# RWKV attention with an expert layer on one core: other fillers on TensorE at the start, and the loads from item 3 on in half rows

## The chip, the cores and the metric

The program runs on one core of a Trainium2 chip. Its time is device microseconds of one execution, as the median over several runs. Engine names are those of the profile: PE is TensorE's products, PEld its loads of weights, DVE is VectorE, ACT ScalarE, POOL GpSimd, and SP the engine that here issues most transfers. A q behind a name means the engine's queue of issues.

## What is computed

An RWKV-5 attention is followed by a mixture of eight experts, all in float32.

```python
# attention: batch 4, 8 heads, 768 tokens, 48 values per head
for t in range(S):
    cur = np.einsum('bhd,bhe->bhde', u[None] * kt, vt)
    y[:, :, t] = np.einsum('bhd,bhde->bhe', rt, state + cur)
    state = w[None, :, :, None] * state + np.einsum('bhd,bhe->bhde', kt, vt)
# experts: x is y as (batch, token, 384); one expert e per token
    e = argmax(logits) if (s == 0 or local_gate < 0.5) else previous e
    h = np.maximum(x[b, s] @ w1[e], 0.0)          # 384 -> 1024
    out[b, s] = p[e] * (h @ w2[e])                # 1024 -> 384
```

## The kernel before, in words

Attention is cut into 16 **items**: one batch and one pair of heads each, four pairs for each of four batches. An item's 768 tokens are six chunks of 128. Within a chunk the recurrence is a matrix of scores; between chunks a state of 48 x 48 per head is carried. The work of an item, with the names that the profile shows:

- `load(n)` issues on SP the transfers of r and k by columns of heads (`rk`, 128 x 1536 values, 768 KB), of keys and values by tokens (`kv`, 128 x 1168, 584 KB) and of the values turned (`vT`, 128 x 768, 384 KB). There are four buffers for `rk` and `vT` and five for `kv`. Items 0 to 2 are loaded ahead of everything; item n + 3 is issued at the head of step n.
- `scale(n)` is POOL's share: `pd` = r times k (L219), `ke` = keys times powers of w to the end of the chunk (L215), and `rw` = r times powers of w (L236). For the items 0 to 2 DVE makes `rw`. Each of the three is two instructions. From item 3 on the order is rw, ke, pd, with item 4 as ke, rw, pd.
- `keys(n)` makes `kw` = k over powers of w on DVE (L246), and on POOL for the last two items.
- On PE: `scores` multiplies rw and kw into a pair of banks (L297), which DVE masks into `am` (L299); `own` is the token's own term, from pd and u (L276), and DVE multiplies it by vT (L282); `added` makes what each chunk adds to the state, from ke and v (L258), which DVE's scan `S` (L264) carries on; `inside` (L306) and `before` (L319) are the two products that make y; ACT copies y out (L327), and `turn` (L338) transposes it.

The powers of w stand in `tab` (and `end`, `endT`), made at the start from `w_t`, which holds w and u for the four pairs of heads. For pair 0 DVE makes them by a scan and for the three others POOL by doubling (L134). `ends` and `turn_ends` make the powers counted from the chunk's end: copies on ACT, two transposes on PE for each pair of heads (L175), and a copy of the result on ACT (L176).

Ahead of item 0's scores PE does **fillers** that nothing reads: `align(26)` is 26 products of 32 x 32, `warm(8)`, `warm(5)` and, ahead of `added(0)`, `warm(3)` are transposes of the unit matrix. A product in float32 is two loads of weights and two products in the profile's counts, a transpose one of each. `banks` hands out two pairs of PSUM banks by turns, to fillers too, so that a tenant waits until the one before the last has been read.

The order of the work is the order in which it is written, for each engine by itself; waits are set by what an instruction reads and overwrites. Besides, every transfer of SP and ACT takes one of eight semaphores by turns, and its issue waits until the transfer that had the semaphore before has landed.

The experts follow. Their tokens are collected by indirect transfers (`xg`) in POOL's queue, the weights `w1t` and `w2t` come by SP and ACT, and the products are L1159, L1209, L1246, L1278 and others.

Of the kernel before, what the change touches and what calls it, by code (L numbers as in the profile page):

```python
# [20 lines left out]
P = 128  # L21
B, H, S, DH = 4, 8, 768, 48
HP = H // 2
DP = 64
# [28 lines left out]
VB = NCH * 2 * DH  # L53
# [3 lines left out]
def spread(ap, axis, n):  # L57

    a = ap.unsqueeze(axis)
    return a.to_broadcast([n if i == axis else s for i, s in enumerate(a.shape)])  # L60


class Attention:
# [13 lines left out]
    def __init__(self, tc, st, rk_d, kv_d, vT_d, x_d, w_t, wp_d, kept, ident, lt, mp):  # L77
        self.tc, self.nc = tc, tc.nc
        nc = tc.nc
        self.rk_d, self.kv_d, self.vT_d, self.x_d = rk_d, kv_d, vT_d, x_d  # L80
        self.w_t, self.kept, self.ident, self.lt = w_t, kept, ident, lt

        self.late = st.enter_context(tc.tile_pool(name="late", bufs=1))
        self.wp = self.late.tile([P, H, 32], F32, name="wp")
        self.inner = ExitStack()

        def pool(name, bufs, **kw):
            return self.inner.enter_context(tc.tile_pool(name=name, bufs=bufs, **kw))

        once = pool("once", 1)  # L90
        self.two = pool("two", 2)
        self.four = pool("four", 4)
        self.py = pool("py", 1, space=PSUM)
        ps = pool("ps", 1, space=PSUM)

        self.pairs = [ps.tile([P, 2, 512], F32, name=f"pair{i}") for i in range(2)]

        self.T = mp[:, 2 * P + 2:2 * P + 2 + (NCH - 1) * DH].rearrange("p (e c) -> p e c", c=NCH - 1)

        self.inv = pool("pinv", 1, space=PSUM).tile([P, HP, P], F32, name="inv")  # L100


        n = B * HP - 1
        self.rks, self.vTs = [None] * AHEAD, [None] * AHEAD
        for i in range(1, AHEAD + 1):
            self.rks[(n + i) % AHEAD] = once.tile([P, 2, NCH, P], F32, name=f"rk{i}")
        for i in range(1, AHEAD + 1):
            self.vTs[(n + i) % AHEAD] = once.tile([P, 2, C2, P], F32, name=f"vT{i}")
        self.kvs = [once.tile([P, 2 * VB + DP - DH], F32, name=f"kv{i}") for i in range(AHEAD + 1)]
        self.items = [dict() for _ in range(B * HP)]  # L110
        self.xTs, self.xs, self.lTs = {}, {}, {}
        for i in range(AHEAD - 1):
            self.load(i)
        nc.sync.dma_start(out=self.wp, in_=wp_d)


        self.step = once.tile([P, HP, DH, NCH - 1], F32, name="step")
        nc.vector.memset(self.step, 0.0)


        self.tab = tab = once.tile([P, HP, 2, P + 1], F32, name="tab")
        nc.vector.memset(tab[:, 0, :, 0:1], 1.0)
        nc.gpsimd.memset(tab[:, 1:, :, 0:1], 1.0)
        w = once.tile([P, HP, 2], F32, name="w")
        nc.vector.tensor_scalar(w[:, :, 0], w_t[:, :, 0], W_LO, W_HI, Alu.max, Alu.min)
        nc.vector.reciprocal(w[:, :, 1], w[:, :, 0])
        none = self.step[:, 0, 0, 0:1].to_broadcast([P, P])
        for o in range(2):
            nc.vector.tensor_tensor_scan(tab[:, 0, o, 1:], w[:, 0, o:o + 1].to_broadcast([P, P]), none, 1.0, Alu.mult, Alu.add)
        nc.gpsimd.tensor_copy(tab[:, 1:, :, 1], w[:, 1:])  # L130
        n, t = 2, tab[:, 1:]
        while n <= P:
            m = min(n - 1, P + 1 - n)
            nc.gpsimd.tensor_mul(t[..., n:n + m], t[..., 1:1 + m], t[..., n - 1:n].to_broadcast([P, HP - 1, 2, m]))  # L134
            n += m

        self.first, self.newton = mp[:, :P + 1], mp[:, P + 1:2 * P + 1]
        nc.scalar.copy(self.first, tab[:, 0, 0])
        self.reciprocals(0)

        self.end = once.tile([P, HP, P + DP], F32, name="end")
        self.endT = once.tile([P, 2, HP, 2 * DH], F32, name="endT")
        self.align(26)
        self.warm(8)
        self.ends(slice(0, 1))
        self.turn_ends(slice(0, 1))
        self.warm(5)

    def align(self, n):

        t = self.banks("warm")
        for i in range(n):
            self.nc.tensor.matmul(t[:32, i % 2, :32], lhsT=self.ident[:, :32], rhs=self.ident[:, :32], start=True, stop=True)

    def reciprocals(self, i):

        nc, inv = self.nc, self.tab[:, i, 1, 1:]
        nc.vector.scalar_tensor_tensor(self.newton, self.first[:, 1:], -1.0, inv, Alu.mult, Alu.mult)
        nc.vector.scalar_tensor_tensor(self.inv[:, i], self.newton, 2.0, inv, Alu.add, Alu.mult)

    def warm(self, n):

        t = self.banks("warm")
        for i in range(n):
            self.nc.tensor.transpose(t[:, i % 2, :P], self.ident, self.ident)

    def ends(self, z):
        self.nc.scalar.copy(self.end[:, z, :P], self.tab[:, z, 0, P - 1::-1])
# [22 lines left out]
    def load(self, n):  # L191
        nc = self.nc
        b, hp = divmod(n, HP)
        rk, vT, kv = self.rks[n % AHEAD], self.vTs[n % AHEAD], self.kvs[n % (AHEAD + 1)]
        if n:
            nc.sync.dma_start(out=rk.rearrange("p a c t -> p (a c t)"), in_=self.rk_d[b, hp])
        else:
            for z in (slice(0, C2), slice(C2, NCH)):
                nc.sync.dma_start(out=rk[:, :, z], in_=self.rk_d[b, hp].rearrange("p (a c t) -> p a c t", a=2, c=NCH)[:, :, z])
        nc.sync.dma_start(out=kv, in_=self.kv_d[b, hp])  # L200
        nc.sync.dma_start(out=vT.rearrange("p a c t -> p (a c t)"), in_=self.vT_d[b, hp])
        self.items[n].update(b=b, hp=hp, rT=rk[:, 0], kT=rk[:, 1], vT=vT,
                             k=kv[:, :VB].rearrange("p (c x) -> p c x", c=NCH), v=kv[:, VB:])
# [158 lines left out]
    def run(self, router, fetch, heads):  # L362
# [11 lines left out]
        for n in range(M + 1):  # L374
            if n + AHEAD - 1 < M:
                self.load(n + AHEAD - 1)
            if n == 0:
                self.scale(0)
                self.keys(0)
                self.tables()  # L380
                self.scores(0, 0)()
                self.scores(0, 1)()
                self.nc.scalar.copy(self.first, self.tab[:, 1, 0])
                self.reciprocals(1)
                self.own(0)
                self.turn_ends(slice(1, HP))
                self.warm(3)
                self.added(0)
                self.states(0)
                self.scale(1)  # L390
                continue
# [133 lines left out]
def general_attention(tc, rk_d, kv_d, wu, wg_d, x_d, ident, lt):  # L525

    nc = tc.nc
    with tc.tile_pool(name="g1", bufs=1) as g1, tc.tile_pool(name="g2", bufs=2) as g2, \
# [8 lines left out]
        nc.vector.tensor_copy(turned[:, DP:], ident[:, :DP])  # L537
        with tc.For_i(0, HP, 1) as hp:
            wu_t = g1.tile([P, 2], F32, name="g_wu")
            nc.sync.dma_start(out=wu_t, in_=wu[bass.ds(hp, 1)].rearrange("o p x -> (o p) x"))  # L540
            with tc.For_i(0, B, 1) as b:
                def of(ap):
                    return ap[bass.ds(b, 1), bass.ds(hp, 1)].rearrange("o q p x -> (o q p) x")
# [7 lines left out]
                                  in_=of(kv_d)[:, 2 * NCH * DH:4 * NCH * DH])  # L551
                yp = gy.tile([P, 2, 512], F32, name="g_y")
                for e in range(DH):
                    vp = gps.tile([P, 2, 512], F32, name="g_vp")
                    for c in range(NCH):
                        for i in range(2):
                            nc.tensor.matmul(
                                vp[i * DP:(i + 1) * DP, c // 3, (c % 3) * P:(c % 3 + 1) * P],
                                lhsT=v_t[:, c, i, e:e + 1].to_broadcast([P, DP]),
                                rhs=turned if c % 2 else ident,  # L560
                                start=True, stop=True)
                    kv = g2.tile([P, S], F32, name="g_kv")
# [6 lines left out]
                    z = g2.tile([P, S], F32, name="g_z")  # L569
                    nc.vector.scalar_tensor_tensor(z, kv, wu_t[:, 1:2], sv[:, :S], Alu.mult, Alu.add)  # L570
                    nc.vector.tensor_mul(z, z, r_t)
                    for c in range(NCH):
                        o = (c % 3) * 2 * DH + 2 * e
                        nc.tensor.matmul(yp[:, c // 3, o:o + 2], lhsT=z[:, c * P:(c + 1) * P], rhs=ones,
                                         start=True, stop=True)
                y = g1.tile([P, 2, 3, 2, DH], F32, name="g_ys")
                for g in range(2):
# [5 lines left out]
                    out=x_d.rearrange("(b c p) (h j) -> b h p c j", b=B, p=P, h=HP)  # L583
                    [bass.ds(b, 1), bass.ds(hp, 1)].rearrange("o q p c j -> (o q p) c j"),
                    in_=y.rearrange("p g c i e -> p (g c) (i e)"))
    with tc.tile_pool(name="g3", bufs=2) as g3, tc.tile_pool(name="gl", bufs=3, space=PSUM) as gl:
        wg = g3.tile([P, DK, E + 1], F32, name="g_wg", bufs=1)
        nc.sync.dma_start(out=wg, in_=wg_d)
        for c in range(NC):
            x = g3.tile([P, D], F32, name="g_x")  # L590
# [7 lines left out]
            for kk in range(DK):  # L598
                nc.tensor.matmul(lp[:, :E + 1], lhsT=xT[:, kk * P:(kk + 1) * P], rhs=wg[:, kk, :],
                                 start=(kk == 0), stop=(kk == DK - 1))  # L600
# [362 lines left out]
def route(tc, once, ps, lt, ident, gates):  # L963
# [57 lines left out]
    nc.vector.tensor_copy(ccol, cp[:NC, :1])  # L1021
    run = tl("run", [NC, P])
    nc.vector.tensor_tensor_scan(run, rows, rows, ccol, Alu.max, Alu.max)
    rp = bank("rp")
    nc.tensor.transpose(rp[:, :NC], run, ident[:NC, :NC])
    ei = tl("ei", [P, NC], I32)
    nc.vector.tensor_copy(ei, rp[:, :NC])
# [635 lines left out]
def kernel(  # L1663
# [12 lines left out]
    nc = tc.nc  # L1676
# [2 lines left out]
    x_d = dram.tile([N, D], F32, name="x_d")  # L1679

    w_t = keep.tile([P, HP, 2], F32, name="w_t")
    nc.scalar.dma_start(out=w_t, in_=wu.rearrange("h p x -> p h x"))
    ident = keep.tile([P, P], F32, name="ident")
    make_identity(nc, ident)
    mask = keep.tile([P, P], F32, name="mask")
# [120 lines left out]
```

## Time and profile before

| | us |
|---|---|
| median of 3 runs | 377.63 |
| lowest and highest | 376.92 and 379.44 |
| the profiled execution, its own time | 378.4 |
| its span, first to last instruction | 376.7 |
| mean granted clock of TensorE | 0.996 |

The profiled execution is a run of its own, 0.8 us above the median; 1.7 us of it lie outside the span. The profile's rows name a line of the kernel, an engine, an operation, what is written and read (buffer numbers left out) and how many instructions were merged into the row (x). In a timeline the first two numbers are the start from the span's beginning and the duration, in us, and the bracket at the end is idle time of that engine just ahead, with what ended it; "issue" stands for a wait for nothing that the profile shows. In a row of the windows an engine has its busy time and, in brackets, its number of instructions; behind the engines come the granted clock, the share of time that the 16 DMA engines were busy, and what they moved.

### The profile page before, as it was taken

The page shows a single profiled execution, that of the slowest core. Times are in us where ns is not written, and L with a number is a line of the kernel's source. Part 1 is how long each engine was busy: PE and PEld are TensorE (multiplying, and loading weights), DVE is VectorE, ACT ScalarE, POOL GpSimd, SP SyncE. Part 2 cuts the span into 40 slices and gives each one's busy share as a digit, 9 for nine tenths or more (in the row PEclk, how much of TensorE's full clock was granted, in tenths as well). Part 3 has the DMA queues.
Part 4 walks back from the last instruction along what each step waited for, and adds up shares of the span by engine and source line. Part 5 has one row for each costly group of instructions (what it writes and reads, how often), then busy time and mean ns, then how long its engine had stood idle before and what let it go on. Part 6 is the DMA issues. An engine that isn't in the chain of part 4 may idle for free. (4 is left out here: it accounts for less than half of the span.)

```text
span 376.7 us, 9667 instructions
## 1 busy us (share of the span) xinstructions
PE 361.5 (96%) x3844; PEld 318.7 (85%) x3844; DVE 244.8 (65%) x711; ACT 110.5 (29%) x304; POOL 152.3 (40%) x212
## 2 busy tenths in 40 slices
PE   7998899999999999999999999999999999999992
PEld 6766777777769998989899999999999998989971
DVE  6887778788834835886557666857767767555300
ACT  4222232223523212322332233333243233331210
POOL 8789999789512055212333113313233023021012
PEclk9999999999999999999999999999999999999998
DMA  7999998992568748713352452264165065072011
GB/s 256 411 407 408 404 409 314 338 357 106 196 194 298 269 169 336 260 35 127 121 198 62 155 216 78 56 218 186 36 209 220 14 220 202 19 259 114 2 41 37
DMA packets 17764, 74.93 MB, mean 199 GB/s; under 512 B 2778, under 2 KB 6624, under 8 KB 15408
## 3 DMA queue, kind: packets, MB, share of 16 engines
q1 hardware_dynamic: 10336, 56.89, 40.7%
q0 software_dynamic: 3424, 9.48, 7.3%
q10 hardware_dynamic: 3952, 7.87, 5.6%
q8 instruction: 32, 0.52, 0.6%
q14 instruction: 20, 0.16, 0.1%
HBM read 64.79 MB, written 9.47 MB: 197 GB/s over the span
## 5 line engine op out<-in xcount | busy, mean ns | idle before, releaser
L1358 POOL DMA_INDIRECT out_dram<-yo,sid x27 | 26.6, 985 | 115.8 <-ACT yo L1353 92.3
L1209 PE MATMUL h<-exT,w1t 128*128 128x168 f32 (+4 forms) x240 | 54.9, 327 | 0.0
L1213 DVE TENSOR_TENSOR hT<-h,hs 128x168 f32<-128x168 f32 (+3 forms) x60 | 21.1, 351 | 46.2 <-PE h L1209 29.6
L1132 POOL DMA_INDIRECT xg<-x_d,gid x29 | 31.2, 1076 | 30.3 <-DVE gid L899 19.2
L1209 PEld LDWEIGHTS h<-exT,w1t 128*128 128x128 f32 x240 | 41.6, 190 | 0.3 <-issue 0.3
L1159 PE MATMUL h<-exT,w1t 128*128 128x168 f32 (+2 forms) x192 | 37.3, 332 | 0.0
L299 DVE TENSOR_TENSOR am<-pair,kept 128x768 f32<-128x768 f32 x32 | 30.1, 953 | 11.0 <-PE pair L297 10.8
L1278 PE MATMUL y<-factors,sums 128*128 128x192 f32 x168 | 36.8, 326 | 0.0
L219 POOL TENSOR_TENSOR pd<-rk 128x384 f32<-128x384 f32 x32 | 31.8, 1014 | 8.9 <-PE y L276 6.3
L1209 PE MATMUL h<-xs,ws 128*128 128x168 f32 (+4 forms) x144 | 35.3, 327 | 0.0
L1159 PEld LDWEIGHTS h<-exT,w1t 128*128 128x128 f32 x192 | 30.9, 190 | 2.0 <-issue 0.2
L1278 PEld LDWEIGHTS y<-factors,sums 128*128 128x128 f32 x168 | 29.0, 190 | 0.2
L1209 PEld LDWEIGHTS h<-xs,ws 128*128 128x128 f32 x144 | 25.5, 190 | 4.3 <-ACT hs L1216 1.2
L297 PE MATMUL pair<-rw,kw 48*64 48x128 f32 (+1 forms) x768 | 23.4, 249 | 1.9 <-issue 1.7
L236 POOL TENSOR_TENSOR rw<-rk,tab 128x384 f32<-128x384 f32 x26 | 23.6, 930 | 0.4 <-DMA rk<-in_rk_dram 0.4
L306 PE MATMUL y<-am,kv 128*64 128x128 f32 x360 | 22.9, 276 | 0.3
L1278 PE MATMUL y<-w2t,hT 128*128 128x192 f32 x96 | 23.0, 328 | 0.0
L297 PEld LDWEIGHTS pair<-rw,kw 48*64 48x64 f32 x768 | 19.9, 133 | 3.4 <-issue 2.4
L1146 DVE COPY exT<-tp 128x384 f32<-128x384 f32 (+5 forms) x29 | 13.8, 485 | 13.2 <-PE tp L1145 13.1
L215 POOL TENSOR_TENSOR ke<-kv,endT 128x288 f32<-128x288 f32 (+1 forms) x32 | 21.8, 704 | 0.9 <-DMA kv<-in_kv_dram 0.9
L306 PEld LDWEIGHTS y<-am,kv 128*64 128x64 f32 x360 | 19.4, 137 | 2.2 <-issue 1.1
L327 ACT COPY xT<-y 128x768 f32<-128x768 f32 x15 | 12.0, 801 | 29.0 <-PE y L319 29.0
(304 smaller groups left out, 735.4 us busy)
## 6 DMA issues: line engine op xcount, KB each, us to landing
w1t<-in_w_dram SPq DMA_DIRECT2D x8, 1536.0 KB, 6.9
w2t<-in_w_dram SPq DMA_DIRECT2D x8, 1536.0 KB, 7.4
rk<-in_rk_dram SPq DMA_DIRECT2D x15, 768.0 KB, 10.3
kv<-in_kv_dram SPq DMA_DIRECT2D x16, 584.0 KB, 8.5
vT<-in_vT_dram SPq DMA_DIRECT2D x16, 384.0 KB, 6.3
x_d<-x ACTq DMA_DIRECT2D x4, 1152.0 KB
w1t<-in_w_dram SPq DMA_DIRECT2D x2, 768.0 KB
w2t<-in_w_dram SPq DMA_DIRECT2D x2, 768.0 KB, 5.2
```

The lines of the kernel that those rows point to most:

```text
L215: nc.gpsimd.tensor_mul(t["ke"][:, z], t["k"][:, z], spread(self.endT[:, p, hp], 1, len(range(NCH)[z])))
L219: nc.gpsimd.tensor_mul(t["pd"][:, z], t["rT"][:, z], t["kT"][:, z])
L236: engine.tensor_mul(t["rw"][:, z], t["rT"][:, z], spread(pw, 1, z.stop - z.start))
L297: nc.tensor.matmul(sc[f * DP:(f + 1) * DP, h, i, x:], lhsT=t["kw"][q, c, o * DP:(o + 1) * DP], rhs=t["rw"][q, c, x:], start=True, stop=True)
L299: return lambda: nc.vector.tensor_mul(t["am"][:, g], sc, spread(self.kept[:, g:g + 3], 1, 2))
L306: nc.tensor.matmul(t["y"][h][p * DP:(p + 1) * DP, c2 * P:(c2 + 1) * P], lhsT=t["v"][:, (2 * c + h) * DH:(2 * c + h) * DH + DP], rhs=t["am" ...
L1132: self.nc.gpsimd.indirect_dma_start(out=xg[:n], out_offset=None, in_=self.x_d[:rows], in_offset=bass.IndirectOffsetOnAxis(ap=u["gid"][:n, ...
L1159: nc.tensor.matmul(h[:, :n], lhsT=u["w1"][:, m, kk, :], rhs=u["xT"][:, kk, :], start=(kk == 0), stop=(kk == DK - 1))
L1209: nc.tensor.matmul(out, lhsT=a, rhs=b, start=start and k == 0, stop=stop and k == len(terms) - 1, skip_group_check=True)
L1213: nc.vector.tensor_tensor(out, a, b, op=Alu.add)
L1278: return lambda: nc.tensor.matmul(bank[:, x * half:(x + 1) * half], lhsT=a, rhs=b, start=(j == 0 and x == 0), stop=(j == FK // 2 - 1), ski ...
L1358: self.nc.gpsimd.indirect_dma_start(out=out.rearrange("n (h d) -> (n h) d", h=2) if half else out, out_offset=bass.IndirectOffsetOnAxis(ap ...
```

## The change

Three things change.

The fillers are now products of the unit matrix with three copies of itself, 384 columns wide: three ahead of the two transposes for pair 0 and one behind. The three transposes ahead of `added(0)` go, and the six transposes of the other pairs move ahead of `own(0)`.

From item 3 on `rk` comes as two transfers, r and then k, and `kv` as two, keys and then values. The rows are then 3,072 bytes for r and k, 2,304 for keys and 2,368 for values, where they were 6,144 and 4,672. `vT` stays whole.

The array of w and u is laid out by partition on the host, so that each partition reads 32 bytes in one piece; before it read four pieces of 8 bytes.

```diff
-        self.align(26)
-        self.warm(8)
+        self.fill(3)
         self.ends(slice(0, 1))
         self.turn_ends(slice(0, 1))
-        self.warm(5)
+        self.fill(1)
...
+    def fill(self, n):
         t = self.banks("warm")
         for i in range(n):
-            self.nc.tensor.matmul(t[:32, i % 2, :32], lhsT=self.ident[:, :32], rhs=self.ident[:, :32], start=True, stop=True)
+            self.nc.tensor.matmul(t[:, i % 2, :3 * P].rearrange("p (c t) -> p c t", c=3), lhsT=self.ident,
+                                  rhs=spread(self.ident, 1, 3), start=True, stop=True)
...
-        if n:
+        if n > 2:
+            for a in range(2):
+                nc.sync.dma_start(out=rk[:, a].rearrange("p c t -> p (c t)"), in_=self.rk_d[b, hp][:, a * S:(a + 1) * S])
+            for a in range(2):
+                z = slice(a * VB, VB if a == 0 else 2 * VB + DP - DH)
+                nc.sync.dma_start(out=kv[:, z], in_=self.kv_d[b, hp][:, z])
+        elif n:
             nc.sync.dma_start(out=rk.rearrange("p a c t -> p (a c t)"), in_=self.rk_d[b, hp])
...
-        nc.sync.dma_start(out=kv, in_=self.kv_d[b, hp])
+        if n <= 2:
+            nc.sync.dma_start(out=kv, in_=self.kv_d[b, hp])
...
                 self.reciprocals(1)
+                self.turn_ends(slice(1, HP))
                 self.own(0)
-                self.turn_ends(slice(1, HP))
-                self.warm(3)
                 self.added(0)
...
-    nc.scalar.dma_start(out=w_t, in_=wu.rearrange("h p x -> p h x"))
+    nc.scalar.dma_start(out=w_t, in_=wu)
...
-        "wu": _np.stack([w, u.reshape(HP, P)], 2),
+        "wu": _np.stack([w, u.reshape(HP, P)], 2).transpose(1, 0, 2),
```

PE's first rows before the change. `pair` is one of the two pairs of banks, with its number; x26 counts the products as the kernel writes them:

```order
1 L153 MATMUL pair_149<-ident 32x32 x26
2 L165 MATMUL pair_148<-ident 128x128 x8
3 L175 MATMUL pair_149<-ident,end 128x128 x2
4 L165 MATMUL pair_148<-ident 128x128 x5
5 L297 MATMUL pair_149<-rw,kw 64x128 x12
6 L297 MATMUL pair_148<-rw,kw 64x128 x12
7 L276 MATMUL y<-pd,w_t 64x384 x4
8 L175 MATMUL pair_149<-ident,end 128x128 x6
9 L165 MATMUL pair_148<-ident 128x128 x3
10 L258 MATMUL mp<-kv_162,ke 64x48 x10
```

And the same place of PE's program after it (the lines of the source have moved):

```order
1 L152 MATMUL pair_149<-ident 128x384 x3
2 L169 MATMUL pair_148<-ident,end 128x128 x2
3 L152 MATMUL pair_149<-ident 128x384
4 L298 MATMUL pair_148<-rw,kw 64x128 x12
5 L298 MATMUL pair_149<-rw,kw 64x128 x12
6 L169 MATMUL pair_148<-ident,end 128x128 x6
7 L277 MATMUL y<-pd,w_t 64x384 x4
8 L259 MATMUL mp<-kv_162,ke 64x48 x10
```

The first scores still take the banks that the two transposes used, and `own(0)` now stands behind the other six transposes.

SP's loads of the items 3 and 4 before the change, with what each issue waits for; DMAHW0 to 7 are the eight semaphores of the transfers:

```order
11 L196 DMA rk_157<-in_rk_dram 128x1536 [waits DMAHW4_49]
12 L200 DMA kv_165<-in_kv_dram 128x1168 [waits DMAHW5_49]
13 L201 DMA vT_161<-in_vT_dram 128x768 [waits DMAHW6_49]
14 L196 DMA rk_154<-in_rk_dram 128x1536 [waits DMAHW7_49,DVE_49,Pool_49]
15 L200 DMA kv_166<-in_kv_dram 128x1168 [waits DMAHW0_49]
16 L201 DMA vT_158<-in_vT_dram 128x768 [waits DMAHW1_49,DVE_49]
```

And after it:

```order
11 L191 DMA rk_157<-in_rk_dram 128x768 [waits DMAHW4_49]
12 L191 DMA rk_157<-in_rk_dram 128x768 [waits DMAHW5_49]
13 L194 DMA kv_165<-in_kv_dram 128x576 [waits DMAHW6_49]
14 L194 DMA kv_165<-in_kv_dram 128x592 [waits DMAHW7_49]
15 L202 DMA vT_161<-in_vT_dram 128x768 [waits DMAHW0_49]
16 L191 DMA rk_154<-in_rk_dram 128x768 [waits DMAHW1_49,DVE_49,Pool_49]
17 L191 DMA rk_154<-in_rk_dram 128x768 [waits DMAHW2_49]
18 L194 DMA kv_166<-in_kv_dram 128x576 [waits DMAHW3_49]
19 L194 DMA kv_166<-in_kv_dram 128x592 [waits DMAHW4_49]
20 L202 DMA vT_158<-in_vT_dram 128x768 [waits DMAHW5_49,DVE_49]
```

An item is five transfers where it was three, and each still waits for the eighth before it.

More of the change, by code (lines that the diff above doesn't have):

```diff
@@ L142, in __init__ @@
         self.endT = once.tile([P, 2, HP, 2 * DH], F32, name="endT")
-        self.align(26)
-        self.warm(8)
+        self.fill(3)
         self.ends(slice(0, 1))
         self.turn_ends(slice(0, 1))
-        self.warm(5)
-    def align(self, n):
+        self.fill(1)
+    def fill(self, n):
         t = self.banks("warm")
         for i in range(n):
-            self.nc.tensor.matmul(t[:32, i % 2, :32], lhsT=self.ident[:, :32], rhs=self.ident[:, :32], start=True, stop=True)
+            self.nc.tensor.matmul(t[:, i % 2, :3 * P].rearrange("p (c t) -> p c t", c=3), lhsT=self.ident,
+                                  rhs=spread(self.ident, 1, 3), start=True, stop=True)
     def reciprocals(self, i):
@@ L159, in reciprocals @@
         nc.vector.scalar_tensor_tensor(self.inv[:, i], self.newton, 2.0, inv, Alu.add, Alu.mult)
[L161 to L165, printed above, removed]
     def ends(self, z):
@@ L539, in general_attention @@
             wu_t = g1.tile([P, 2], F32, name="g_wu")
-            nc.sync.dma_start(out=wu_t, in_=wu[bass.ds(hp, 1)].rearrange("o p x -> (o p) x"))
+            nc.sync.dma_start(out=wu_t, in_=wu[:, bass.ds(hp, 1)].rearrange("p o x -> p (o x)"))
             with tc.For_i(0, B, 1) as b:
```

## The prediction

> **What bounds the kernel now.** I read the windows first, since the program has two stages with different limits.
>
> ```profile
> core 0: us, PE busy (x) PEld busy (x) DVE busy (x) ACT busy (x) POOL busy (x), PEclk, DMA share, GB/s
> 3.00:4.00 1.00, 1.00 (x23) 1.00 (x22) 0.95 (x4) 0.26 (x2) 0.51 (x3) 1.00 1.00 307
> 10.00:15.00 5.00, 5.00 (x125) 4.49 (x126) 3.95 (x7) 1.61 (x3) 3.62 (x5) 1.00 1.02 415
> ...
> 200.00:300.00 100.00, 100.00 (x630) 95.23 (x629) 69.14 (x229) 32.24 (x91) 24.67 (x31) 1.00 0.38 134
> ```
>
> From 200 to 300 us PE is busy all the time, with DMA at 0.38: the experts are bound by products. Nothing in the change touches them, so what it is worth is how much earlier or later attention hands over to them. Up to 57 us the picture is another: the 16 DMA engines have no free time (share 1.02). An item is 768 + 584 + 384 KB, 1.78 MB, so 4.4 us at 408 GB/s. The timeline of POOL shows who waits for these loads, that of PE who does not:
>
> ```profile
> 8.79 1.55 POOL L215 TENSOR_TENSOR ke<-kv,endT 128x288 f32<-128x288 f32 x2
> 11.34 1.96 POOL L219 TENSOR_TENSOR pd<-rk 128x384 f32<-128x384 f32 x2 [1.01 <-DMA rk<-in_rk_dram]
> 16.02 1.97 POOL L219 TENSOR_TENSOR pd<-rk 128x384 f32<-128x384 f32 x2 [1.39 <-DMA rk<-in_rk_dram]
> 20.63 1.69 POOL L236 TENSOR_TENSOR rw<-rk,tab 128x384 f32<-128x384 f32 x2 [0.42 <-DMA rk<-in_rk_dram]
> 23.59 1.97 POOL L219 TENSOR_TENSOR pd<-rk 128x384 f32<-128x384 f32 x2
> 26.49 1.35 POOL L215 TENSOR_TENSOR ke<-kv,endT 128x288 f32<-128x288 f32 x2 [0.94 <-DMA kv<-in_kv_dram]
> 45.49 1.97 POOL L219 TENSOR_TENSOR pd<-rk 128x384 f32<-128x384 f32 x2 [0.81 <-PE y L276]
> ```
>
> POOL waits for loads of items 1 to 4 only. From 26.49 it needs 1.69 + 1.35 + 1.97 = 5.0 us an item, more than the 4.4 us of a load, so the loads run ahead; at 45.49 its first later wait is for PE. And PE, in the timeline of its weight loads, stands still in the middle of groups with no releaser:
>
> ```profile
> 26.77 0.54 PEld L297 LDWEIGHTS pair<-rw,kw 48*64 48x64 f32 x23 [0.44 <-issue]
> 33.43 0.54 PEld L297 LDWEIGHTS pair<-rw,kw 48*64 48x64 f32 x22 [1.09 <-issue]
> 39.77 0.30 PEld L258 LDWEIGHTS mp<-kv,ke 128*48 128x48 f32 x9 [1.47 <-issue]
> 51.93 0.48 PEld L258 LDWEIGHTS mp<-kv,ke 128*48 128x48 f32 x17 [0.52 <-issue]
> 57.53 0.44 PEld L258 LDWEIGHTS mp<-kv,ke 128*48 128x48 f32 x16 [0.24 <-issue]
> ```
>
> The windows cut at these halts (and at 46.0, where no halt is seen) count what PE did between them:
>
> ```profile
> 26.76:33.42 6.66, 5.64 (x126) 4.47 (x127) 5.82 (x7) 1.50 (x3) 6.66 (x9) 1.00 1.02 408
> 33.42:39.76 6.34, 4.99 (x126) 3.11 (x125) 4.61 (x6) 0.48 (x1) 6.34 (x8) 1.00 1.03 412
> 39.76:46.00 6.24, 6.23 (x126) 4.97 (x126) 3.60 (x23) 1.50 (x3) 5.42 (x8) 1.00 1.01 399
> 45.99:51.92 5.93, 5.54 (x130) 4.37 (x129) 4.86 (x7) 2.94 (x12) 5.86 (x8) 1.00 1.04 410
> 51.92:57.52 5.60, 5.48 (x126) 4.32 (x127) 3.93 (x6) 1.22 (x3) 4.64 (x6) 1.00 1.03 409
> 57.52:62.60 5.08, 5.07 (x125) 3.81 (x128) 4.17 (x7) 1.21 (x3) 4.72 (x7) 1.00 0.93 344
> ...
> PE 361.5 (96%) x3844; PEld 318.7 (85%) x3844; DVE 244.8 (65%) x711; ACT 110.5 (29%) x304; POOL 152.3 (40%) x212
> ...
> q1 hardware_dynamic: 10336, 56.89, 40.7%
> q10 hardware_dynamic: 3952, 7.87, 5.6%
> q8 instruction: 32, 0.52, 0.6%
> ```
>
> Products and weight loads add up to 251 to 259 each time, and the DMA queue called instruction moved 32 pieces, 0.52 MB / 32 = 16 KB each. PE ran 3,844 + 3,844 instructions, 240 for each of 32 pieces. I infer that PE's program comes in pieces of about 256 instructions through the same busy DMA engines, and that while these are full a piece takes 5.6 to 6.7 us to come. So **from 20 to 57 us PE is paced by its own program**; the halts add up to 0.44 + 1.09 + 1.47 + 0.52 + 0.24 = 3.8 us. At DMA share 0.93 the piece takes 5.08 us and nothing halts.
>
> **The change, part by part.** *The front on PE.* The rows of the start:
>
> ```profile
> 1.55 2.98 PE L153 MATMUL pair<-ident 128*32 128x32 f32 x52 [1.55 <-POOL ident masks.py:199]
> 3.01 0.17 DVE L125 TENSOR_SCALAR w<-w_t 128x4 f32<-128x4 f32 x1 [1.05 <-DMA w_t<-in_wu_dram]
> 4.46 1.17 PE L165 MATMUL pair<-ident 128*128 128x128 f32 x8
> 5.69 0.71 PE L165 MATMUL pair<-ident 128*128 128x128 f32 x5
> 6.31 0.55 DVE L236 TENSOR_TENSOR rw<-rk,mp 128x384 f32<-128x384 f32 x1
> 6.33 1.54 PE L297 MATMUL pair<-rw,kw 48*64 48x128 f32 x48
> 10.39 0.49 PE L165 MATMUL pair<-ident 128*128 128x128 f32 x3
> 10.81 0.79 PE L258 MATMUL mp<-kv,ke 128*64 128x48 f32 x20
> ...
> 252.25 0.81 PE L1285 MATMUL tp<-w2t,hT 128*120 128x384 f32 x2
> 252.90 0.32 PE L1209 MATMUL h<-xs,ws 128*128 128x188 f32 x1
> ```
>
> A product of 384 columns in f32 is two instructions; the pair at 252.25 held PE for 0.65 us. Three fillers end at 1.55 + 1.95 = 3.5 us, against 5.4 for the old ones, which held back the two transposes behind them. Their copy frees the bank for the first scores, which can then start when the first half of rw is there (5.9) instead of 6.33. That does not carry far: the second half of rw ends at 6.86 as before. Then the three transposes at 10.39 go, and own(0) changes places with the six transposes of the other pairs of heads. What is late next for the added states (10.81) is ke(0), which POOL ends at 10.34: they start at 10.4, a gain of **0.4 us** for PE and for DVE's scan behind them. own(0) still waits for pd(0), and DVE's product behind it isn't moved.
>
> *w and u by whole rows of a partition.* 512 pieces of 8 bytes become 128 of 32. DVE waits 1.05 us for them, so the gain lies between 0 and 1.05 at the start of the tables. What is late next is rk(1), 1.01 us on POOL at 11.34, which this does not bring; nearest to that row I take 0. The same edit in the general path is not executed.
>
> *The half rows.* No byte more. Added per item: two issues on SP, 26 in all, and 256 rows, 16 for each DMA engine. What a row costs beside its bytes the trace bounds from two sides. The window from 3 to 4 us moves the 1,536-byte rows of item 0 at 307 GB/s, 80 ns a row per engine, against 59 at 415: at most 21 ns, 0.34 us an item. The queue table gives 0.407 x 6,027 us / 10,336 = 237 ns at 5,504 bytes a packet and 0.056 x 6,027 / 3,952 = 85 ns at 1,991 bytes: a line through both has no fixed part. The new rows (2,304 to 3,072 bytes) lie between these two, so I take 0, and keep 0.34. The issues:
>
> ```profile
> 11.29 0.33 SPq L200 DMA_DIRECT2D kv<-in_kv_dram  x1
> ...
> rk<-in_rk_dram SPq DMA_DIRECT2D x15, 768.0 KB, 10.3
> kv<-in_kv_dram SPq DMA_DIRECT2D x16, 584.0 KB, 8.5
> ```
>
> 0.33 us each, beside 10.3 us from issue to landing: hidden while loads run ahead; 8.6 us on SP if they did not. Eight loads may be on their way (each waits for the eighth before it, as the order shows): by the mean of an item that was 8/3 x 1.78 = 4.7 MB, 11.6 us at 408 GB/s, and becomes 8/5 x 1.78 = 2.8 MB, 7 us: still enough to keep the engines full, and without that cover each wait of SP would show.
>
> What the halves bring: rw needs r alone, ke keys alone. r of item 3 lands 384 KB, 0.96 us, before the whole would, so the wait of 0.42 at 20.63 goes, and late next is POOL itself. Keys of item 4 land 296 KB, 0.74 us, earlier: ke(4) starts at 26.49 - 0.74 = 25.75, and POOL is free by then. POOL gains **0.7 us** (0.1 at 0.34 us an item for two items).
>
> *What of it reaches the end.* PE, paced by its program, decides. Its instructions get 68 products and as many loads fewer and 8 and 8 more: 120 fewer, about half a piece, so each halt falls 120 instructions later. The gain of 0.4 us on PE reaches the stretch; POOL's 0.7 us reaches it where PE waits for ke or rw. Where the halts now fall can save up to half of a middling halt (0.5) or cost as much. I take 0.4 + 0.3 = **0.7 us** off, with ends at +0.5 and -1.4. Sum: 378.4 - 0.7 = 377.7 for the profiled execution. That one is 0.8 above the median of the runs, 377.63, so the forecast on the median is 376.9.
>
> A rule of the Trainium skill speaks against the halves. "DMA: Bandwidth & Descriptors", section "Rules for kernel authors", asks for at least 1 MiB a transfer, and its fit (section on the anatomy of one DMA) gives each a fixed part of about 2.0 us. Put end to end, two more transfers would add 4 us to an item; the trace does not agree that they stand end to end (10.3 us to landing, 4.4 us an item).
>
> **The rivals.** *Halves move slower* (0.06). If short transfers run at the 307 to 343 GB/s of item 0's halves, take 330, an item takes 5.4 us, more than POOL's 5.0. ke(4) comes 2 x 1.0 - 0.7 = 1.3 us later, and DMA stays full to 20.6 + 12 x 5.4 = 85 us instead of 57, so some four more pieces halt at the mean of 3.8 / 5 = 0.75 us: 377.6 - 0.4 + 1.3 + 3.0 = 381.5. It decides from about 355 GB/s downwards, where an item takes POOL's 5.0 us. Against it: the 3,072-byte rows of vT, 384 KB each, already run within the 415. The rule above would act in this way.
>
> *PE's clock falls at the front* (0.05). The fillers may be what holds it. At half speed until about 10 us, scores, own, added and inside of item 0 (1.5 + 0.9 + 0.8 + 1.5) take twice as long; POOL's waits of 1.01 and 1.39 swallow some 2.4 of these 4.7 us: 376.9 + 2.3 = 379.2. Against it: the granted clock reads 1.00 in every window, and the 8 and the 3 transposes run alike. "TensorE: Matmul & The Clock Gate", section "Part 1", states a clock of half speed for the first 3.4 us or so; three fillers would by that end at 5.5 us, which ke(0) hides.
>
> *Program pieces come sooner* (0.18). If a piece waits behind a number of rows, not of bytes, rows of half the length shorten that wait, and most of 3.8 us goes; POOL's 5.0 us an item against PE's 5.3 (5.60 x 240 / 256, an item having some 240 instructions) lets some 2.5 of it through beside the 0.7: 374.4. For it: halts vanish as soon as DMA has gaps. Against it: the pieces' time hardly varies (5.6 to 6.7) with what is loaded.
>
> *It doesn't arrive* (0.16): the halts fix PE's pace, POOL waits for PE instead (0.81 at 45.49 grows), and the time stays, 377.6.
>
> **How the numbers follow.** My forecast, 376.9, has 0.55. The range from 374.0 to 380.0 takes in all but the slow halves and the tails. A change under 1%, 3.8 us, can hardly be told from none here; the runs of before spread over 2.5 us. Faster by more than that needs program pieces that come sooner and more: 0.10. Slower: the slow halves and a little of the clock, 0.07. Within: 0.83.
>
> **What would show it.** Added states of item 0 near 10.4 us; no wait for DMA at rw(3), ke(4) near 25.8; halts on PE still there, of some 0.5 to 1.5 us, 120 instructions later; windows from 10 to 50 us still near 408 GB/s. A rate under 390, halts that are gone, or a POOL that waits for r from item 5 on would prove the steps wrong.

## The result: 1.0 per cent slower, outside the forecast range

| | before | after |
|---|---|---|
| median, us | 377.62 (6 runs) | 382.0 (6 runs) |
| lowest and highest, us | 376.92 and 379.44 | 379.71 and 385.28 |
| ratio, 95% interval | | 1.0104, 1.0065 to 1.0144 |
| profiled execution, its own time and span, us | 378.4 and 376.7 | 383.1 and 381.4 |
| mean granted clock of TensorE | 0.996 | 0.984 |

The forecast was 376.9, with a range to 380.0. The six runs of after go with their granted clock: 379.71 us at 0.996, 382.52 at 0.988, 385.28 at 0.979. The profiled one, 383.1 at 0.984, is 1.1 us above their median, so the account that follows is of a run somewhat longer than the middle one. The handover from attention shows the whole loss: POOL's first gather of tokens for the experts, in the timelines of before and of after, comes 4.2 us later, and behind it PE's distance to before does not grow.

```profile
102.89 1.27 POOL L1132 DMA_INDIRECT xg<-x_d,gid  x1 [3.69 <-DVE gid L899]
```

```profile
107.10 1.27 POOL L1132 DMA_INDIRECT xg<-x_d,gid  x1 [3.70 <-DVE gid L899]
```

**The front.** PE's timeline of after, from the first filler to the added states of item 0:

```profile
1.55 4.21 PE L152 MATMUL pair<-ident 128*128 128x384 f32 x6 [1.55 <-POOL ident masks.py:199]
5.55 0.63 PE L169 MATMUL pair<-ident,end 128*128 128x128 f32 x2
5.98 1.36 PE L152 MATMUL pair<-ident 128*128 128x384 f32 x2
7.27 1.54 PE L298 MATMUL pair<-rw,kw 48*64 48x128 f32 x48
9.43 0.85 PE L169 MATMUL pair<-ident,end 128*128 128x128 f32 x6 [0.62 <-DVE am L300]
10.20 0.88 PE L277 MATMUL y<-pd,w_t 48*64 48x384 f32 x8
11.01 0.79 PE L259 MATMUL mp<-kv,ke 128*64 128x48 f32 x20
```

Six instructions of 384 columns hold PE until 5.55, not 3.5: about 0.64 us each, 1.28 a product. The scores start at 7.27 (6.33 before), the six transposes wait for the bank until DVE has made `am`, and own(0), now behind them, starts at 10.20 (8.88 before). The added states come at 11.01, against 10.81 before and 10.4 in the forecast.

PE is slow there although the clock's column reads 1.00. The trace's first record of the granted clock begins at 4.67 us in before and at 7.08 in after; the column takes the time ahead of it as 1.00. The eight transposes that took 1.17 us in before (4.46, in the prediction's rows) took 1.97 in the run e2 below, which has the same fillers and its first record at 7.16:

```profile
4.47 1.97 PE L165 MATMUL pair<-ident 128*128 128x128 f32 x8
```

In the profiles of this document that record begins anywhere from 4.35 to 7.90 us. e4 below has after's fillers and its record at 5.86; its scores start at 6.67 and its added states at 10.40. So some 0.6 us of after's late front belong to that one execution.

**The loads.** The windows of after, beside 399 to 415 GB/s before from 10 to 57 us in the rows shown ahead:

```profile
20.00:25.00 5.00, 4.68 (x106) 3.57 (x104) 4.81 (x8) 1.77 (x4) 5.00 (x15) 1.00 1.04 392
30.00:40.00 10.00, 9.88 (x229) 7.26 (x227) 8.53 (x12) 2.12 (x5) 10.00 (x13) 1.00 1.04 396
40.00:50.00 10.00, 8.50 (x160) 6.26 (x158) 5.08 (x25) 1.50 (x3) 9.29 (x12) 0.83 1.04 393
```

From 30 to 40 us PE is busy 9.88 of 10 us: the halts of 1.09 and 1.47 that before had there are gone, and where before stands at 40 us PE is 2.3 us ahead, by the same instruction in both traces. From 40 to 50 us the granted clock is 0.83 in the mean. The loads are also issued later: r of item 4 at 18.57 us, where before issued its r and k together at 14.05.

**Where the lead goes.** ACT's timelines, of before and of after:

```profile
40.95 0.70 ACT L340 COPY x<-pair 128x288 f32<-128x288 f32 x2 [4.14 <-PE pair L338]
41.68 0.40 ACTq L343 DMA_DIRECT2D x_d<-x  x1
43.58 0.80 ACT L327 COPY xT<-y 128x768 f32<-128x768 f32 x1 [1.93 <-PE y L319]
```

```profile
38.62 0.70 ACT L341 COPY x<-pair 128x288 f32<-128x288 f32 x2 [2.67 <-DVE am L300]
43.15 0.41 ACTq L344 DMA_DIRECT2D x_d<-x  x1
43.60 0.80 ACT L328 COPY xT<-y 128x768 f32<-128x768 f32 x1 [4.27 <-DMA rk<-in_rk_dram]
```

Before, ACT issued the store of batch 0's x right behind the two copies. After, the copies end at 39.3 and the issue comes at 43.15; the profile puts the 4.27 us down to a load of rk, which ACT does not read. It is the semaphore: the store takes the next of the eight that SP's loads use, and waits for the load that had it. The copy of y stands behind the issue in ACT's queue, and PE waits for that copy (timeline of PE's weight loads), then the windows:

```profile
44.45 0.21 PEld L277 LDWEIGHTS y<-pd,w_t 48*64 48x64 f32 x8 [1.73 <-ACT xT L328]
```

```profile
43.00:44.00 1.00, 0.00 (x0) 0.00 (x0) 0.50 (x1) 0.40 (x1) 1.00 (x3) 1.00 1.05 396
45.00:46.00 1.00, 1.00 (x9) 0.18 (x2) 0.01 (x1) 0.00 (x0) 0.32 (x1) 0.50 1.07 401
47.00:48.00 1.00, 1.00 (x24) 0.87 (x24) 1.00 (x2) 0.70 (x2) 1.00 (x3) 0.50 1.04 391
48.00:49.00 1.00, 1.00 (x24) 1.00 (x22) 1.00 (x2) 0.00 (x0) 1.00 (x2) 0.98 1.05 406
74.00:75.00 1.00, 0.00 (x0) 0.00 (x0) 0.98 (x2) 0.00 (x0) 1.00 (x2) 1.00 1.03 395
76.00:77.00 1.00, 1.00 (x30) 1.00 (x25) 0.00 (x0) 0.36 (x1) 0.00 (x0) 0.50 1.01 403
```

PE does nothing from 43 to 44 us and then runs at half its clock for some 3 us; where before stands at 46 us, the lead of 2.3 us has become a lag of 1.2. The same happens again at 74: PE halts for a piece of its program,

```profile
75.16 0.81 PEld L320 LDWEIGHTS y<-rw,S 48*48 48x48 f32 x17 [1.97 <-issue]
```

while DMA is full (1.03), and the clock is at 0.50 from 76 on. From there the lag is some 4.2 us, to the end.

### The profile page after: what moved, and what is told of

It reads as the page before. It is cut to its first block, busy times and chain, and to the rows that moved or that the text cites. A ratio compares the mean times of both kernels' runs of the same rounds, so it can differ in the third digit from the quotient of the medians.

```text
span 381.4 us, 9580 instructions
## 1 busy us (share of the span) xinstructions
PE 365.4 (96%) x3784; PEld 319.0 (84%) x3784; DVE 245.0 (64%) x711; ACT 110.3 (29%) x304; POOL 152.3 (40%) x212
```

## The experiments

The ratios are to the kernel before, timed beside each on the same chip; its medians there were 377.81 (e1 to e4), 378.22 (e5 to e8), 378.17 (e9 to e12) and 377.40 us (e13 to e15). "Candidate" is the kernel before with the new layout of w and u, and ACT's store written behind its copy of y.

**Each part alone.** e1_fillers is before with the new fillers and their order, e2_halves with the half rows, e3_wu with the new layout of w and u (each of them the hunks shown above); e4_after_xlate is the whole change, with

```diff
-        (in turn) nc.scalar.dma_start(out=self.x_d[...], in_=x)
             self.before(n - 1)
+            nc.scalar.dma_start(out=self.x_d[...], in_=x)   # of the batch that turn has just ended
```

> The kernel before with the new fillers and the new order of own(0) alone; loads and w and u as before. If the loss sits in the fillers (scores of item 0 at 7.3 us instead of 6.3, and the program's pieces cut 120 instructions later), this is some 2 to 4 us slower than before. If it sits in the half rows, this is within 1 us of before: 377 to 379, and its granted clock stays at 0.99 or more.

> The kernel before with the half rows alone. If the transfer of x to memory in ACT's queue waits for a load of SP, because the eight semaphores are shared and the eighth transfer before it is now a later load, ACT's copy of y stands behind it as in the changed kernel, PE idles for 1 to 2 us and the clock halves after that: 380 to 382. If the fillers are to blame, this is 376.5 to 377.5, with the pieces of PE's program coming 1 us sooner.

> The kernel before with the new layout of w and u alone. Every theory expects little: DVE starts up to 0.6 us earlier, POOL then waits for rk of item 1 as before. 377.0 to 377.8.

> The changed kernel, with the transfer of x to memory written behind the copy of y (L328) instead of ahead of it in ACT's program. If ACT's wait for a shared semaphore is the cause of the idle PE at 43 us, the wait now holds nothing up, the copy follows its products at about 42.8 us, no half clock follows at 44 to 48 us, and the time falls by about 3 us to 379, further if the second place is of the same cause. If the fillers or the pieces of the program are to blame, it stays at 381 to 382.

| | median, us | ratio, 95% interval |
|---|---|---|
| e1_fillers | 381.22 | 1.0088, 1.0053 to 1.0124 |
| e2_halves | 379.93 | 1.0055, 1.0030 to 1.0079 |
| e3_wu | 377.42 | 0.9989, 0.9970 to 1.0007 |
| e4_after_xlate | 379.55 | 1.0041, 1.0021 to 1.0062 |

Fillers and half rows each cost time by themselves. The three ratios add up to 1.3 per cent. The change cost 1.0, which the intervals do not tell apart from that; e4, with all three parts and ACT's issue moved, cost 0.4, so the parts do not simply add. Moving ACT's issue took 0.6 per cent, some 2.4 us, off the change. After's own fastest run, with its clock at 0.996, took 379.71 us, about e4's median. That suggests, without proving it, that the wait costs time in the main through the falls of the clock. ACT's timeline of e4 shows the copy of y no longer waiting for a load:

```profile
41.80 0.80 ACT L329 COPY xT<-y 128x768 f32<-128x768 f32 x1 [2.99 <-PE y L321]
43.45 0.41 ACTq L345 DMA_DIRECT2D x_d<-x  x1
```

The store itself goes no earlier (43.45 against 43.15); only what stands behind it is free.

**The front, or the places of the program's pieces?** e6_place_only has 120 instructions of PE fewer, as the change has, but keeps the front's time and order.

```diff
-        self.align(26)
-        self.warm(8)
+        self.fill(2)
+        self.warm(2)
         self.ends(slice(0, 1))
         self.turn_ends(slice(0, 1))
-        self.warm(5)
+        self.warm(2)
...
-                self.warm(3)
                 self.added(0)
```

> The kernel before with 120 fewer instructions of PE in the front, as in the change, but fillers of the old duration (two products of 384 columns and two transposes, 2.9 us at the half speed that the trace of after shows, in place of 4.1), and own(0) still ahead of the six transposes. PE's program pieces so begin at the instructions where they begin after the change, while the front's times stay as before. Theory 'the places of the pieces decide': added(0) at 10.8 as before, no halt ahead of 41 us and PE some 2 us ahead there, then halts at about 41, 47, 54 and of over 1 us at about 73 and 80 us; 379.2 to 380.5, that is the loss of the fillers alone (381.2) less the 0.6 us that these lose in the front. Theory 'the late front decides' (scores(0) 0.7 us late, own(0) behind the transposes): 377.6 or less.

It took 381.35, ratio 1.0073 (1.0045 to 1.0101). The added states come at 10.30, 0.5 us ahead of before, and PE is 2.8 us ahead at 40 us. The timelines of PE and of its weight loads:

```profile
10.30 0.79 PE L265 MATMUL mp<-kv,ke 128*64 128x48 f32 x20
```

```profile
41.27 0.24 PEld L326 LDWEIGHTS y<-rw,S 48*48 48x48 f32 x2 [0.50 <-issue]
47.58 0.16 PEld L326 LDWEIGHTS y<-rw,S 48*48 48x48 f32 x1 [0.81 <-issue]
54.18 0.15 PEld L326 LDWEIGHTS y<-rw,S 48*48 48x48 f32 x1 [1.18 <-issue]
73.06 0.56 PEld L326 LDWEIGHTS y<-rw,S 48*48 48x48 f32 x17 [0.61 <-issue]
79.30 0.68 PEld L326 LDWEIGHTS y<-rw,S 48*48 48x48 f32 x20 [0.69 <-issue]
86.19 0.13 PEld L313 LDWEIGHTS y<-am,kv 128*64 128x64 f32 x1 [1.42 <-issue]
```

The halts ahead of 41 us are nearly gone, others come, up to 86 us, and its gather starts 2.5 us later than before's. An early front did not help, so the late front is not what cost the time. e6 still has two wide fillers; some of the next runs have none.

**Other places.** e8, e9 and e10 are the candidate (e7) with other mixes of fillers; e14 and e15 have 11 and 22 small products more, at the head of own(0), where PE waits for pd(0); e13 has two wide fillers and as many small products there as bring the pieces back to where before has them. e6, in the table with them, has neither the new layout of w and u nor the moved store.

```diff
         (in own, ahead of its products)
+        if n == 0:
+            for i in range(11):     # 22 in e15, 18 in e13
+                nc.tensor.matmul(y[:32, i % 2, :32], lhsT=self.ident[:, :32], rhs=self.ident[:, :32], start=True, stop=True)
```

> A candidate: the kernel before with w and u by whole rows of a partition, and ACT's store of x issued behind its copy of y. Old fillers, whole rows. If the layout of w and u brings a little (its run alone gave 0.9989) and the store never blocks ACT in the kernel before (x's transfer there takes a semaphore that is free 0.4 us after the copies), 377.0 to 377.5. If ACT's wait costs something in the kernel before as well, 376.5 or less.

> The candidate with the program pieces at a third place: one product of 384 columns and 14 small ones in place of the 26 small ones (2.9 us as before), 44 instructions fewer. Theory 'the places decide': the halts of PE fall at other instructions, and the time differs from the candidate's by up to 2 us in either direction with no other change in the front. Theory 'the places do not matter': the same as the candidate within 0.5 us.

> The candidate (w and u by partitions, ACT's store of x behind its copy of y, whole rows, old order) with the program pieces at yet another place: two products of 384 columns and 3 small ones in place of the 26 small ones, 84 instructions fewer. Theory 'the places decide': the time lies somewhere between the candidate's (0.998 of before) and that of the pieces where the change has them (1.007), and PE's halts stand at other instructions. Theory 'wide fillers cost the time by themselves': 1.007 or more, since two of the four wide products are here.

> The candidate with 15 small products and 16 transposes in place of 26 and 8: 28 instructions fewer, no wide filler at all. Theory 'the places decide': up to 2 us from the candidate's time in either direction. Theory 'wide fillers cost the time': the candidate's time within 0.5 us.

> The candidate (w and u by partitions, ACT's store of x behind its copy of y) with wide fillers at the start (two products of 384 columns, seven small ones, six transposes: 72 instructions fewer), and 18 small products directly ahead of own(0) that nothing reads (72 instructions), where PE waits 1 us for pd(0). From own(0) on the program pieces stand where the kernel before has them. Theory 'the places decide': the candidate's time (0.998 of before), up to 0.5 us more for products that outlast the wait. Theory 'wide fillers decide': 1.005 or more, as the kernel with 84 instructions fewer that has the same two wide products.

> The candidate with 11 small products more, ahead of own(0) where PE waits: 44 instructions more, so every piece of PE's program begins earlier in the work. Theory 'the places decide': another time than the candidate's, in either direction, by up to 2 us. If each instruction fewer costs (0.9979 at none, 1.0004 at 28, 1.0007 at 44, 1.0051 at 84, 1.0073 at 120), more of them gain: 0.995.

> As the one with 44 instructions more, with 22 small products, 88 more. Theory 'the places decide': a third time; if each instruction more gained, 0.992 to 0.995; and some 0.3 us lost ahead of own(0), since 44 small products may outlast the wait for pd(0).

| | PE instructions ahead of item 0's states | wide fillers | median, us | ratio, 95% interval |
|---|---|---|---|---|
| e6_place_only | -120 | 2 | 381.35 | 1.0073, 1.0045 to 1.0101 |
| e9_place_84 | -84 | 2 | 380.13 | 1.0051, 1.0023 to 1.0078 |
| e8_wu_xlate_place | -44 | 1 | 379.69 | 1.0007, 0.9976 to 1.0038 |
| e10_place_28 | -28 | 0 | 378.54 | 1.0004, 0.9975 to 1.0034 |
| e7_wu_xlate | 0 | 0 | 378.19 | 0.9979, 0.9956 to 1.0002 |
| e13_wide_old_place | 0 | 2 | 379.63 | 1.0042, 1.0012 to 1.0072 |
| e14_place_plus44 | +44 | 0 | 380.97 | 1.0102, 1.0069 to 1.0135 |
| e15_place_plus88 | +88 | 0 | 382.58 | 1.0146, 1.0118 to 1.0174 |

e14 has no wide filler, and its front keeps its time: the added states of item 0 start at 10.72 us, against 10.81 in before. It is 1.0 per cent slower. Its weight loads on PE:

```profile
26.59 0.97 PEld L301 LDWEIGHTS pair<-rw,kw 48*64 48x64 f32 x43 [0.93 <-issue]
32.89 0.97 PEld L301 LDWEIGHTS pair<-rw,kw 48*64 48x64 f32 x43 [0.69 <-issue]
39.13 0.30 PEld L301 LDWEIGHTS pair<-rw,kw 48*64 48x64 f32 x10 [1.56 <-issue]
45.46 0.14 PEld L301 LDWEIGHTS pair<-rw,kw 48*64 48x64 f32 x3 [1.04 <-issue]
51.79 0.14 PEld L301 LDWEIGHTS pair<-rw,kw 48*64 48x64 f32 x2 [1.06 <-issue]
```

The halts stand 6.2 to 6.3 us apart, as long as a piece takes to come, and there are two of over 1 us at 45 and 51 where before had none and one of 0.52. So 1 per cent is lost without a wide filler and without a late front. Not all of it need be the places: where a piece of some 252 instructions takes 6.3 us, 44 instructions more are 1.1 us by an estimate from these rows, and no run separates the two. e10, 28 instructions fewer and no wide filler, cannot be told from the candidate, which is what the rival 'wide fillers' expected; e9, with two of them, lies at 1.0051 where that rival had 1.007. That fewer instructions cost and more gain, which I had read from the first five rows, fell with e14 and e15. e13 remains between: with the pieces put back, its first halts stand at the very instructions of before, with the same numbers of weight loads behind them (x23, x9),

```profile
27.40 0.54 PEld L309 LDWEIGHTS pair<-rw,kw 48*64 48x64 f32 x23 [0.44 <-issue]
40.12 0.30 PEld L267 LDWEIGHTS mp<-kv,ke 128*48 128x48 f32 x9 [1.47 <-issue]
82.25 0.13 PEld L309 LDWEIGHTS pair<-rw,kw 48*64 48x64 f32 x1 [0.96 <-issue]
```

yet it is slower than the candidate. Some 0.6 us of that is its front (the small products outlast the wait), and the halt at 82.25 is larger than before's 0.65 at 80.39. So e13 lies between the two rivals, the places (the candidate's time and up to 0.5 us more) and the wide fillers (1.005 or more), and its interval takes in the second. Whether wide fillers cost anything besides is open.

**What the half rows cost.** e12_rk_rows brings r and k as one transfer with rows of 3,072 bytes. e5_by_partition brings as many transfers as the change, with whole rows, cut by partitions. e11_halves_wu_xlate is the candidate with the half rows.

```diff
-            nc.sync.dma_start(out=rk.rearrange("p a c t -> p (a c t)"), in_=self.rk_d[b, hp])
+            (e12, r and k apart in DRAM) nc.sync.dma_start(out=rk.rearrange("p a c t -> p a (c t)"), in_=self.rk_d[b, hp].rearrange("a p s -> p a s"))
+            (e5, and kv likewise) for q in (slice(0, DP), slice(DP, P)):
+                nc.sync.dma_start(out=rk[q].rearrange("p a c t -> p (a c t)"), in_=self.rk_d[b, hp][q])
```

> The kernel before, with rk and kv from item 3 on as two transfers each, but cut by partitions (64 whole rows of 6,144 or 4,672 bytes) in place of columns. As many transfers, issues and semaphores as with half rows, and the long rows of before. Theory 'the shorter rows cost the rate': 10 to 50 us is back at 404 to 415 GB/s, no new halts of PE at 58 and 65 us, 377.6. Theory 'the number of transfers costs it' (fewer bytes on their way, since eight transfers are 2.8 MB now): 393 to 397 GB/s and the halts at 58 and 65 us as with half rows, 379.9.

> The change without its front: half rows, the layout of w and u, ACT's store of x behind its copy of y, and the old fillers and order. If the half rows cost time only by what they do to the loads' rate and to the halts at 58 and 65 us, as half rows alone do (1.0055), 1.004 to 1.006 less what w and u bring: 379.0 to 380.0. If ACT's blocked store was part of that loss too, 377.5 to 378.5.

> The kernel before, with r and k laid out apart in DRAM, so that rk comes as one transfer as before, but in rows of 3,072 bytes (items 1 and 2 too); keys and values as before. Three transfers an item, 128 rows more. Theory 'a row costs beside its bytes': by the packets' time of half rows (14,080 packets at 41.2% against 10,336 at 40.7%, some 16 ns for each row more) half the loss of rate, so 399 to 403 GB/s from 20 to 50 us against 404 to 410, and about 1 us slower. Theory 'the number of transfers costs the rate': 404 to 410 GB/s and the time of before.

| | median, us | ratio, 95% interval |
|---|---|---|
| e5_by_partition | 415.28 | 1.0955, 1.0911 to 1.0999 |
| e11_halves_wu_xlate | 379.98 | 1.0063, 1.0026 to 1.0100 |
| e12_rk_rows | 379.53 | 1.0038, 1.0013 to 1.0064 |

The window from 20 to 25 us, of e2 (half rows), of e12 and of e5:

```profile
20.00:25.00 5.00, 4.65 (x101) 3.40 (x98) 4.49 (x8) 1.74 (x4) 5.00 (x16) 1.00 1.04 396
```

```profile
20.00:25.00 5.00, 4.61 (x105) 3.72 (x104) 4.66 (x9) 1.77 (x4) 4.77 (x9) 1.00 1.02 399
```

```profile
20.00:25.00 5.00, 4.12 (x78) 3.10 (x80) 3.89 (x7) 1.06 (x4) 1.15 (x6) 1.00 1.02 201
```

e12, with three transfers an item as before, runs at 399 to 402 GB/s up to 40 us, between before (403 to 410) and the half rows (395 to 396): rows cost. From 408 to 395.5 GB/s an item of 1.78 MB takes 0.14 us longer, 9 ns for each of its 16 more rows an engine; e12, at 400 with 8 more rows an engine, gives some 11 ns. What the 0.4 per cent consist of that e12 lost in time is not settled: w_t came 2 us late in its profiled execution, and its front with it. e5 was meant to tell rows from transfers and told something else (last section).

The rate itself is not what the half rows cost most. The weight loads of e2 show the halts of before, and where DMA is still full they are larger, with a new one:

```profile
58.62 0.44 PEld L265 LDWEIGHTS mp<-kv,ke 128*48 128x48 f32 x16 [0.79 <-issue]
64.89 0.15 PEld L357 LDWEIGHTS pair<-xT,wp 128*32 128x32 f32 x5 [1.07 <-issue]
```

Before had 0.24 at 57.53 and none after it until 80.39. From 60 to 65 us the DMA share is 1.00 in e2 and 0.83 in before. e11 shows the same two, 0.78 and 0.79 us, and its time says that ACT's store had no part in this loss. Nor did the halves bring what they were for. In after and e2 POOL no longer waits for r at rw(3), but it still waits for keys at ke(4), 0.93 and 0.96 us, and starts that at 27.16 and 26.76, later than before's 26.49. POOL's timeline of e11 has both waits,

```profile
20.85 1.69 POOL L244 TENSOR_TENSOR rw<-rk,tab 128x384 f32<-128x384 f32 x2 [0.48 <-DMA rk<-in_rk_dram]
27.16 1.35 POOL L223 TENSOR_TENSOR ke<-kv,endT 128x288 f32<-128x288 f32 x2 [1.20 <-DMA kv<-in_kv_dram]
```

where before waited 0.42 and 0.94.

No version beats both kernels for certain. The candidate e7 beats the kernel after; against before, its interval takes in no change, and its median, 378.19, is that of before beside it, 378.22.

## Why the prediction was wrong, step by step

**What bounds the kernel** held from 20 to 57 us: PE's pace there is that of its program, and halts of the same kind come up to 86. The traces say more than the prediction used. They time each packet of the queue called instruction, and in the 17 profiles PE stood still without a releaser, for 0.25 us or more, 85 times from 17 to 95 us: each of these halts ended 1.2 to 1.7 us after a packet of 16 KB had landed in that queue. That PE waits for these pieces is thereby shown. Why a full DMA makes them late is not: the packet itself takes 1.08 us (median) from 17 to 57 us and 1.12 from 200 to 300, where before has DMA at 0.38. e14, which adds 22 product instructions of 0.04 us to a wait, and with them moves where pieces begin, costs 1 per cent, which a bound by loads or products would not.

**"What of it reaches the end"** is the step that failed first. It sized the move of the halts at half of a middling halt, 0.5 us either way. Yet 120 of some 252 instructions, at 6.3 us a piece, are 3.0 us by an estimate from the prediction's own rows. By the traces PE was 2.5 us ahead where before stands at 40 us in e1, whose added states start when before's do, and 2.8 in e6; at the end e1 was 2.1 behind. All kernels with moved pieces lie between 1.0004 and 1.0146. The working priced each halt by itself and asked whether it falls earlier or later. What it left out is that halts go on after 57 us, up to 86, where a piece comes while DMA is full or nearly so: before had one of 0.65 in that stretch, e6 has three, of 0.61, 0.69 and 1.42, with DMA at 0.73 to 1.06 from 70 to 85 us. Which pieces meet a full DMA is what 120 instructions decide; that reading is from the traces, and no run takes the other transfers away to prove it.

**"Eight loads may be on their way ... still enough"** looked at SP alone. There it held: the DMA share stayed at 1.04 from 20 to 50 us, though r of item 4 was issued 4.5 us later than before's r and k. The eight semaphores are also those of ACT's stores, as the description of the kernel says, and five transfers an item change which load a store waits for. With PE ahead of its loads, ACT stood 3.8 us at that issue. Nothing in the sum had a term for it; e4 measures it at 2.4 us, PE's slower clock included.

**The half rows** were priced at 0 a row, with 0.34 us an item as the upper bound; measured is 0.14. The gain of 0.7 us on POOL did not come. It took for granted that r and keys would be issued when the whole arrays were, and that the rate would stay; both failed, as above. The rival "halves move slower" had the right mechanism, a DMA that stays full longer and so later pieces that halt. Its rate (330) and its point (355) were far off: 395 was enough.

**The front**: a filler was priced by the pair at 252 us, deep in the experts, and runs at half that speed at the start. The rule of the Trainium skill that stood beside it ("TensorE: Matmul & The Clock Gate", section "Part 1") gave 5.5 us for the end of three fillers, and the trace shows that end. I had let the granted clock of 1.00 in every window speak against it; that column does not show the half speed at the start, as it has no record there. And ke(0) did not hide it: the scores come 0.9 us late, and own(0) waits behind the transposes for the bank. e6, with shorter fillers and the old order, has the added states at 10.30, and e4, with after's fillers and an earlier full clock, at 10.40. That is the 10.4 of the forecast, but by luck: the fillers were as slow as the rival had them.

**w and u**: 0 was taken. DVE has them at 2.43 to 2.52 us in all but one of the profiles with the new layout (2.71 in e11), and at 2.81 to 3.01 with the old one, in e12 at 5.01. That is some 0.4 us on DVE, and 0.9989 in time tells nothing from no change.

## What to carry to other kernels

Where an engine's program comes through the DMA engines that the loads keep full, adding or taking away a hundred instructions anywhere ahead moves every halt behind; measure a change of fillers at two or three other counts before crediting it or blaming it. A store on one engine's queue that shares semaphores with another engine's loads belongs behind everything that others wait for. And an idle PE can cost twice, since the clock may fall with it: each wait of 1.9 us or more from 8 to 105 us brought that here.

## What the runs showed of the hardware

- *The clock.* PE's waits of 1.73 us at 44.45 and 1.97 us at 75.16 were each followed by about 3.4 us at half the granted clock, and so was one of 1.96 us in e8. All six waits of 1.9 to 4.2 us in these traces, from 8 to 105 us, had such a fall; in the four of them in e5, of 3.2 us and more, it came while PE still waited and lasted 6.8 to 10.2 us, two or three times 3.4. Of the twelve from 1.4 to 1.8 us, two had one (1.73 in after, 1.42 in e12) and ten had none, one of 1.73 in e5 among them. The Trainium skill ("TensorE: Matmul & The Clock Gate", section "Part 1") has the clock fall after an idle window of some 3.4 us, and the window run freely. The length of the slow stretch and the chance in it agree; the idle time that set it off in after and e8 is about half as long.
- *Partitions.* Loads into partitions 0 to 63 and then 64 to 127 moved 201 to 214 GB/s from 20 to 40 us, with the DMA engines busy all the time, against 408 to 410 for whole tiles. The kernel took 37 us longer, six stretches at half the granted clock (41 us in all) included. "SBUF — State Buffer" of the Trainium skill, section "Door 1", says that 64 such partitions reach 8 of 16 ports; the halved rate agrees.
